# One maximum over two PSUM banks, batchwise reciprocals and a regrouped weight ring in an attention plus two-network kernel

## Chip, core and metric

One core of one Trainium2 chip. The metric is the device time of one execution in microseconds; lower is better. All stage times below come from one profiled execution of the kernel before.

## The reference

A causal attention with a decay bias (4 batches, 8 heads, 576 tokens, 64 elements a head) feeds a first feed-forward network, and that a second (512 to 2,048 to 512 elements, 2,304 tokens), all in float32:

```python
scores = scale * np.matmul(q, k.transpose(0, 1, 3, 2))
cum = np.cumsum(np.maximum(s, 0.0), axis=-1)
bias = -(cum[:, :, :, None] - cum[:, :, None, :])
scores = np.where(causal, -1000000000.0, scores + np.minimum(bias, 0.0))
attn = np.exp(scores - np.max(scores, axis=-1, keepdims=True))
attn = attn / (np.sum(attn, axis=-1, keepdims=True) + 1e-09)
x = np.matmul(attn, v)          # then (2304, 512)
h = x @ w_in;  x = (h * np.cos(h)) @ w_out
h = x @ w2_in; out = (np.maximum(h, 0.0) + np.log1p(np.exp(-np.abs(h)))) @ w2_out
```

## The kernel before

**Order.** A planner written in the kernel (class `Planner`) decides the order of everything. Each operation is an `Op` with a due value `vt`, the engines it can run on, and the tiles it reads and writes; `plan` walks through modelled time and gives each free engine the ready operation with the smallest `vt`, corrected on TensorE by what it thinks a weight load costs (`LDW`, `FX`, `then`). The due values are offsets in the table `TUNE`. Where the model sees TensorE idle, it puts in warm-up matmuls on constants: `warm` (line 415, "fillers") until the first product with v, `warmer` (line 423, tile `still`) later. All transfers are issued by SyncE (SP), one queue, in the planned order, through `dma` at line 312, and every real matmul through `mms` at line 358, so operations are told apart here by tiles and shapes.

**Attention.** `emit_attention` is called for each of the 32 heads. Every head needs its row maxima first, so each causal block is scored twice. In the first pass six matmuls (`MT`, four groups in four PSUM banks) score the five query blocks; the fifth block's 576 keys do not fit one bank of 512 columns and stand as 320 and 256 in two banks. VectorE takes one masked maximum of each piece (line 592, columns of `mx`), and line 598 combines the two of the fifth block into `mrr`. A transpose on TensorE (T, 128 columns), ScalarE (line 615) and GpSimd (line 617) turn the maxima into rows that the second pass subtracts. That pass (`STL`) scores keys by queries in four groups, two matmuls of each width (448; 128 and 320; 448; 192 and 64); ScalarE takes the exponential (line 657), GpSimd zeroes the diagonal halves (line 663), and TensorE multiplies with v, which carries a column of ones: "bank<-gs", fp32, 65 stationary columns, two passes for each of six widths. The rest is fp32r, which a row of the trace also calls f32: every value is split into a high and a low part, and three products replace one. Five of the eight PSUM banks rotate among maxima, transposes and scores (`rot`), three hold the products with v.

**Sums.** The numerator and the sum of each head go to DRAM (`adram<-gs`). After every fourth head the sums come back (`rd<-adram`), are inverted (lines 692, 693) and stored (`rdram<-rd`). `normal` then loads numerators (`uu<-adram`) and broadcast reciprocals (`wo<-rdram`), multiplies them (line 737), stores them (`xnorm<-uu`) for later use, and `emit_x` forms seven sums of blocks and their parts.

**Networks.** Each network is a two-level Strassen scheme with seven products (`PROD`, P1, P5, P6, P2, P3, P7, P4). A unit, "quad", is 42 matmuls of 384 columns with one pair of weight blocks; its weights lie in one of two ring slots (`ring`), loaded by two DMAs `rg<-wd`, a half j = 0 or 1 of 1,792 columns each, and every product needs both. The weights were converted earlier (lines 483, 485, 504, `emit_win`) and stored to `wd` in pieces of 448 KB. The products with w_out (`emit_g2`) are 384 columns wide in the first network ("bank<-rg,wo") and 512 in the second ("bank<-wo,rg", three in a row for each output block).

## Time and profile before

| | us |
|---|---|
| median of 3 runs (lowest, highest) | 959.97 (958.52, 960.05) |
| profiled execution, its span | 958.9, 957.2 |
| TensorE, weight loads, VectorE, ScalarE busy | 946.8, 866.9, 817.2, 713.3 |
| first real matmul | 7.50 |
| first matmul of the first network | 197.52 |
| start of the unbroken run of TensorE, its end | 281.92, 953.3 |

The span is one execution from its first to its last instruction; the profiled execution's own time is 1.7 us longer. Matmuls are pipelined and their records overlap, so a group's busy time says little: distances between starts say more. An idle time stands before the instruction that follows it, with what released it. The granted clock of TensorE is 1.00 in all stages.

### The profile page before, as it was taken

Reading aid. Unit: us, or ns where it says so; the run is one execution under the profiler, and the core shown is the slowest. Engines: PE = TensorE matmul, PEld = TensorE weight load, DVE = VectorE, ACT = ScalarE, POOL = GpSimd, SP = SyncE. Lnnn points to the kernel's source line nnn. Section 1 sums busy time; section 2 is a strip of 40 time slices with the busy share of each in tenths; the row PEclk is TensorE's granted clock in tenths of the full one; section 3 lists DMA queues with packets and bytes.
Section 4 is the critical chain, followed back from the end, with each engine's and each line's share of the span. In section 5 each row is a group of like instructions: output and inputs, shape, how many; then the busy total and the mean of one; then the engine's idle time right before and its main releaser. Section 6 shows DMA issues by size and latency. Waiting matters only on the chain.

```text
span 957.2 us, 15903 instructions
## 1 busy us (share of the span) xinstructions
PE 946.8 (99%) x5162; PEld 866.9 (91%) x5162; DVE 817.2 (85%) x1930; ACT 713.3 (75%) x1502; POOL 98.0 (10%) x220
## 2 busy tenths in 40 slices
PE   8999999999999999999999999999999999999998
PEld 7778878789999999999999999989899998898996
DVE  8898898959989898898897998989977788289685
ACT  5888788768778587885885877869867786377572
POOL 6444444510000000000000000000000000000000
PEclk9999999999999999999999999999999999999999
DMA  6799988988896886789858889776464445146324
GB/s 184 216 258 268 284 261 251 281 291 315 294 323 237 314 313 252 275 300 319 309 212 284 310 290 312 249 258 213 165 228 157 154 155 176 35 167 216 133 78 131
DMA packets 80972, 226.62 MB, mean 237 GB/s; under 512 B 11390, under 2 KB 22654, under 8 KB 80890
## 3 DMA queue, kind: packets, MB, share of 16 engines
q1 hardware_dynamic: 80890, 225.62, 70.0%
q8 instruction: 40, 0.66, 0.3%
q14 instruction: 42, 0.34, 0.1%
HBM read 163.49 MB, written 53.25 MB: 226 GB/s over the span
## 4 chain that ended last, share of the span: by engine, by line
PE 93%; DVE 3%; DMA 2%; SPq 1%; issue 0%; ACT 0%; DVEq 0%; ACTq 0%
PE bank L358 92%; DMA wo<-rdram 1%; SPq L312 1%; PE bank L415 1%; DMA adram<-gs 1%; DMA ae<-rdram 0%; DVE ae L812 0%; DVE gs L592 0%; DMA gs<-s 0%; DVE rg L443 0%; DVE rg L340 0%; DVE gs L438 0%; DVE ae L333 0%; DVE gs L815 0%; DVE ae L815 0%
## 5 line engine op out<-in xcount | busy, mean ns | idle before, releaser
L358 PE MATMUL bank<-xc,rg 128*128 128x384 f32 x2016 | 387.8, 335 | 3.5 <-DMA rg<-wd 2.9
L358 PEld LDWEIGHTS bank<-xc,rg 128*128 128x128 f32 x2016 | 354.4, 188 | 14.7 <-DVE ae L812 2.9
L358 PE MATMUL bank<-rg,wo 128*128 128x384 f32 x1152 | 219.5, 335 | 0.0
L358 PE MATMUL bank<-wo,rg 128*128 128x512 f32 x864 | 214.9, 392 | 0.0
L358 PEld LDWEIGHTS bank<-rg,wo 128*128 128x128 f32 x1152 | 201.1, 188 | 1.3 <-DVE rg L340 0.7
L358 PEld LDWEIGHTS bank<-wo,rg 128*128 128x128 f32 x864 | 160.9, 188 | 26.9
L358 PE MATMUL bank<-gs 128*65 128x448 f32 (+4 forms) x384 | 114.9, 410 | 0.0
L796 DVE TENSOR_TENSOR ae<-bank,ae 128x384 f32<-128x384 f32 x144 | 78.6, 552 | 41.8 <-PE bank L358 40.1
L358 PE MATMUL bank<-rg 128*128 128x448 f32 (+14 forms) x448 | 105.5, 339 | 1.8 <-DVE rg L443 1.0
L331 ACT ACTIVATE ae<-bank 128x384 f32<-128x384 f32 (+1 forms) x136 | 67.4, 499 | 44.2 <-PE bank L358 41.8
L358 PEld LDWEIGHTS bank<-rg 128*128 128x128 f32 (+5 forms) x448 | 65.8, 177 | 25.0 <-issue 11.0
L592 DVE CUSTOM_DVE_ANT_0 gs<-bank,gs 128x320 bf16<-128x320 f32 (+2 forms) x192 | 75.1, 431 | 12.1 <-PE bank L358 10.0
L331 ACT ACTIVATE rg<-gs 128x384 fp32r<-128x384 f32 x96 | 49.4, 520 | 34.9 <-PE bank L358 34.2
L657 ACT ACTIVATE gs<-bank 128x448 f32<-128x448 f32 (+1 forms) x128 | 62.2, 498 | 14.4 <-PE bank L358 9.2
L483 ACT ACTIVATE upper<-stage 128x256 f16<-128x256 bf16 x128 | 61.2, 490 | 15.1 <-DMA stage<-w 7.9
L358 PEld LDWEIGHTS bank<-gs 128*65 128x65 f32 x384 | 60.6, 195 | 5.7 <-POOL gs L663 1.4
L340 DVE TENSOR_TENSOR rg<-gs,rg 128x384 fp32r<-128x384 f32 (+1 forms) x97 | 53.0, 552 | 9.8 <-ACT rg L331 9.7
L820 DVE SCALAR_TENSOR_TENSOR ae<-ae 128x384 f32<-128x384 f32 x96 | 52.8, 553 | 9.0 <-ACT ae L819 8.3
L819 ACT ACTIVATE ae<-ae,lnb 128x384 f32<-128x384 f32 x96 | 58.1, 611 | 1.9
L331 ACT ACTIVATE rg<-ae 128x384 fp32r<-128x384 f32 x96 | 49.6, 518 | 12.4 <-DVE ae L824 9.6
L663 POOL TENSOR_SCALAR_AFFINE_SELECT gs<-gs 128x128 f32<-128x128 f32 (+1 forms) x160 | 53.7, 358 | 42.0 <-ACT gs L657 40.3
L485 DVE SCALAR_TENSOR_TENSOR wt<-stage,upper 128x256 uint32<-128x256 uint32 x128 | 51.6, 417 | 6.9 <-ACT upper L483 6.7
(96 smaller groups left out, 1200.4 us busy)
## 6 DMA issues: line engine op xcount, KB each, us to landing
rg<-wd SPq DMA_DIRECT2D x96, 896.0 KB
stage<-w SPq DMA_DIRECT2D x128, 256.0 KB
wd<-rg SPq DMA_DIRECT2D x48, 448.0 KB
uu<-qk SPq DMA_DIRECT2D x15, 576.0 KB
uu<-xdram SPq DMA_DIRECT2D x20, 384.0 KB
wd<-xc SPq DMA_DIRECT2D x16, 448.0 KB
rg<-rg SPq DMA_DIRECT2D x20, 288.0 KB
gs<-v SPq DMA_DIRECT2D x32, 160.0 KB
```

Of the source, the lines that this page charges most:

```text
L312: (G if by == POOL else nc.sync).dma_start(o, i)
L331: opts.append((ACT, act_t(n, psum), (lambda: A.activation(o, i, AF.Copy, scale=1.0 if scale is None else scale))))
L340: return [(DVE, dve_t(n), lambda: V.tensor_tensor(o, a, hi.bitcast(F32), op=ALU.subtract))]
L358: X.matmul(o, a, b, start=st, stop=sp, skip_group_check=skip)
L483: P.op(vs_ - 1 + 0.1 * z, [(ACT, act_t(256) + 45.0, lambda up=up, head=head: A.activation(up[:, :].bitcast(F16).rearrange("p (n t) -> p n ...
L485: P.op(vs_ + 0.1 * z, [(DVE, dve_t(256), lambda up=up, mid=mid, z=z: V.scalar_tensor_tensor(cv[:, z * 256:z * 256 + 256], mid, 13, up, op0 ...
L592: P.op(tx + 1, [(DVE, dve_t(w, True) + DX, free(lambda bk=bk, off=off, w=w, mo=mo, col=col, pr=pr, jk=junk[i if x < 2 else x - 2]: V.tenso ...
L657: P.op(tx + 3, [(ACT, act_t(wt, True) + AX, lambda pt=pt, bk=bk, wt=wt: A.activation(pt[:, :wt], bank[bk][:, :wt], AF.Exp))], r=[(("bank", ...
L663: P.op(tx + 4 + i, [(POOL, 160.0 + 0.8 * dw, lambda z=pt[:, off:off + dw], dw=dw: G.affine_select(out=z, in_=z, pattern=[[1, dw]], compare ...
L796: P.op(t - 80, [(DVE, dve_t(NQ, True), lambda o=o, e=et[x]: V.tensor_tensor(e, o, e, op=ALU.add))], r=done + [(ek[x], (Q, "s"))], w=[(ek[x ...
L819: P.op(te + 400, [(ACT, act_t(NQ) + 93, lambda a0=a0, a1=a1: A.activation(a1, a0, AF.Ln, bias=lnb[:, 0:1]))], r=[(k0, (tg, "e")), ("ln", 0 ...
L820: P.op(te + 700, [(DVE, dve_t(NQ), lambda a0=a0: V.scalar_tensor_tensor(a0, a0, 2.0, a0, op0=ALU.subtract, op1=ALU.mult, reverse0=True))], ...
```

## The change

- **Planner.** All numbers of `TUNE` are new. A load of v counts `LDW` = 110 ns instead of 54, `FX` is 2.5 instead of 30, and one SP transfer that depends on another becomes ready 1,000 ns later (`dd`).
- **Maxima.** PSUM is one tile of 4,096 columns. The two pieces of the fifth block stand in adjacent banks (`rot` picks the pair), and one operation of 576 columns takes their maximum. All maxima are written into `mrr` directly; `mx` and line 598 are gone.
- **Scores.** `STL` becomes 192 and 256; 320 and 64; 448; 320. The first key block is split 256 and 320 rather than 128 and 448. The first two groups are double-buffered, and the two diagonals of one group are selected in one operation on GpSimd (four a head instead of five).
- **Sums.** They are inverted once for eight heads in the first three batches; in the last batch still for four, the second time with a due value later by `late`.
- **Ring.** `wd` is laid out in two groups (`PART`): 2,048 columns for P1, P5, P6, P2 and 1,536 for P3, P7, P4. Each store to `wd` becomes two. A product waits for its own group alone.
- **Second network.** Inner blocks of w_out issue nine matmuls in one operation (three blocks of three).
- **Start.** The mask is prepared earlier on GpSimd, and two due values (`tz`, `x2nd`) move the first subtractions.

The diff, cut:

```diff
+PART = (2048, 1536)
+POS = (1, 3, 4, 2, 5, 6, 0)
...
-LDW = 107.0
+LDW = 110.0
...
-                        then = 54.0 if len(fast) > (f.load < 100.0) else LDW
+                        then = 30.0 if len(fast) > (f.load < 100.0) else LDW
...
-                    s.ready = max(s.ready, o.end + min(self.hop(e, x[0]) for x in s.opts))
+                    s.ready = max(s.ready, o.end + min(self.hop(e, x[0]) for x in s.opts) + (TUNE["dd"] if e == SP and s.opts[0][0] == SP else 0.0))
...
-AX, DX, FX = 50.0, 12.0, 30.0
+AX, DX, FX = 50.0, 12.0, 2.5
...
-    bank = [pp.tile([128, 512], F32, name=f"bank{i}", tag=f"bank{i}") for i in range(8)]
+    psum = pp.tile([128, 4096], F32, name="bank", tag="bank")
+    bank = [psum[:, i * 512:i * 512 + 512] for i in range(8)]
...
-            loads += [54.0, 0.0] if n < 0 else [max(27.0, st.shape[-1] * LDW / 128)]
+            loads += [LDW, 0.0] if n < 0 else [max(27.0, st.shape[-1] * LDW / 128)]
...
-            dma(t + 4 + z, wdram[which][i, :, j * HALF + z * 896:j * HALF + z * 896 + 896], x.bitcast(F32), r=[(("sh", h, z), tag)], w=[(("wd", which, i, j, z), 0)], by=SP)
+            for g, (a, b) in enumerate(((384, 896), (0, 384))):
+                o = g * PART[0] + (2 * j + z) * (b - a)
+                dma(t + 4 + z + 0.1 * g, wdram[which][i, :, o:o + b - a], x[:, a:b].bitcast(F32), r=[(("sh", h, z), tag)], w=[(("wd", which, i, j, z, g), 0)], by=SP)
...
-    MT = [[(4, 0, 320, 4, 0), (1, 0, 192, 1, 320)], [(3, 0, 448, 3, 0), (0, 0, 64, 0, 448)], [(2, 0, 320, 2, 0)], [(4, 320, 256, 9, 0)]]
-    STL = [[(0, 128, 0, 448)], [(0, 0, 0, 128), (2, 256, 128, 320)], [(1, 128, 0, 448)], [(3, 384, 0, 192), (4, 512, 192, 64)]]
+    MT = [[(1, 0, 192, 0), (4, 0, 320, 192)], [(4, 320, 256, 0), (0, 0, 64, 256)], [(3, 0, 448, 0)], [(2, 0, 320, 0)]]
+    STL = [[(3, 384, 0, 192), (0, 0, 192, 256)], [(0, 256, 0, 320), (4, 512, 320, 64)], [(1, 128, 0, 448)], [(2, 256, 0, 320)]]
+    AVL = [[(0, 0, 128), (3, 384, S)], [(0, 128, S), (4, 512, S)], [(1, 128, S)], [(2, 256, S)]]
...
-                    op0=ALU.add, op1=ALU.max, accum_out=m[0:pr, col:col + 1])))],
-                    r=[(("bank", bk), (bt, len(lst) - 1)), ("mask", 0)], w=[(("mx", sl, col), tg)])
-        t = at(st["max"] + 0.5)
-        mk = ("xl", 1, u % 3)
-        P.op(t, [(DVE, 115.0, lambda: V.tensor_tensor(mrr[:, 96:101], m[:, 0:5], m[:, 5:10], op=ALU.max))],
...
+                    out=jk[0:pr, :w], in0=psum[0:pr, 512 * bk + off:512 * bk + off + w], in1=mask[0:pr, mo:mo + w], scale=1.0, scalar=BIG,
+                    op0=ALU.add, op1=ALU.max, accum_out=mrr[0:pr, 96 + qi:97 + qi])))],
+                    r=[(("bank", bk), (bt, len(lst) - 1)), ("mask", 0)] + ([(("bank", rot[u, "m", 1]), ((tg, "m", 1), 1))] if qi == 4 else []), w=[(mk, tg)])
...
-        if u % 4 != 3:
+        nh = 4 if b == NB - 1 else 8
+        if u % nh != nh - 1:
             return
-        tn = at(st["norm"])
+        tn = at(st["norm"]) + (TUNE["late"] if b == NB - 1 else 0.0)
...
-        for j in range(2):
-            dma(tq - QUAD + 100 + j, ring[r].bitcast(F32)[:, j * HALF:j * HALF + HALF], wdram[which][i, :, j * HALF:j * HALF + HALF],
-                r=[(("wd", which, i, j, z), 0) for z in range(2)], w=[(("ring", r, j), Q)] + first(("ring", r, j)))
+        for g in range(2):
+            gs_ = slice(g * PART[0], g * PART[0] + PART[g])
+            dma(tq - QUAD + 100 + g * TUNE["rg"], ring[r].bitcast(F32)[:, gs_], wdram[which][i, :, gs_],
+                r=[(("wd", which, i, j, z, g), 0) for j in range(2) for z in range(2)], w=[(("ring", r, g), Q)] + first(("ring", r, g)))
...
-                P.op(tq + (y + j / 2) * h, mms(ml), r=[(("ring", r, j), Q)] + [(("xc", xi, j, t), xtag) for t in range(2)] + old, w=[(("bank", b), (Q, nm, j))])
+                P.op(tq + (y + j / 2) * h, mms(ml), r=[(("ring", r, POS[wi] < 3), Q)] + [(("xc", xi, j, t), xtag) for t in range(2)] + old, w=[(("bank", b), (Q, nm, j))])
...
+        if which and f0 < f < f1 - 1:
+            ml = [(bank[yset[m]], (hi, lo)[xt][:, m * 128:m * 128 + 128], wo[:, f, wt_], False, False, False, DM) for m in range(3) for wt_, xt in ((0, 0), (1, 0), (0, 1))]
```


**TensorE, one head in the steady part of the attention.** Names: `gs` with 65 rows of output is the product with v (its outputs' width stands behind the x), `rg` with 128 rows are maxima and scores, 32x128 is T. Before:

```order
L358 MATMUL bank_68<-rg 128x128
L358 MATMUL bank_68<-rg 128x320
L358 MATMUL bank_66<-rg 32x128
L358 MATMUL bank_68<-rg 128x320
L358 MATMUL bank_69<-rg 128x320
L358 MATMUL bank_69<-rg 128x192
L358 MATMUL bank_65<-rg 128x448 x2
L358 MATMUL bank_66<-rg 128x448
L358 MATMUL bank_66<-rg 128x64
L358 MATMUL bank_70<-gs 65x192
L358 MATMUL bank_70<-gs 65x64
L358 MATMUL bank_67<-rg 128x192 x2
```

A head of the steady part on the same engine after the change:

```order
L361 MATMUL bank<-gs 65x192
L361 MATMUL bank<-gs 65x128
L361 MATMUL bank<-rg 128x320
L361 MATMUL bank<-rg 128x256
L361 MATMUL bank<-rg 128x192
L361 MATMUL bank<-rg 128x256 x2
L361 MATMUL bank<-gs 65x448
L361 MATMUL bank<-rg 128x320 x2
L361 MATMUL bank<-gs 65x64
L361 MATMUL bank<-gs 65x448
L361 MATMUL bank<-rg 32x128
```

The two score matmuls of 128 columns (the second of the pair is the first row) are gone, 32x128 aside; the 64-column product with v stands ahead of a 448-column one rather than of a maximum, and the pairs beside the products are 256 or 320 wide.

**SP, at the end of the attention.** `adram<-gs` stores a head, `rd<-adram` reads the sums of the last four heads, `uu` and `wo` load numerators and reciprocals, `rg<-wd` fills the ring, `xnorm<-uu` stores products of VectorE. Before:

```order
L312 DMA adram<-gs 65x576 x2
L312 DMA rg<-wd_78 128x1792
L312 DMA xnorm<-uu 128x768
L312 DMA rd<-adram 128x1x18
L312 DMA uu<-adram 64x768 x2
L312 DMA wo<-rdram 64x768
L312 DMA uu<-adram 64x768 x2
L312 DMA wo<-rdram 64x768 x2
L312 DMA rg<-wd_78 128x1792
L312 DMA rdram<-rd 4x32x18
L312 DMA xnorm<-uu 128x768
L312 DMA rg<-wd_78 128x1792
```

The same queue at the same place after the change:

```order
L315 DMA adram<-gs 65x576 x2
L315 DMA rdram<-rd 4x32x18
L315 DMA rg<-wd_71 128x1536
L315 DMA uu<-adram 64x768 x2
L315 DMA wo<-rdram 64x768 x2
L315 DMA uu<-adram 64x768 x2
L315 DMA wo<-rdram 64x768 x2
L315 DMA uu<-adram 64x768 x2
L315 DMA rg<-wd_71 128x2048
L315 DMA rd<-adram 128x1x18
L315 DMA xnorm<-uu 128x768 x2
L315 DMA wo<-rdram 64x768 x2
L315 DMA rg<-wd_71 128x1536
```

The read `rd<-adram` stood two transfers behind the last heads' stores and ahead of seven loads and both ring loads; now it stands behind ten loads and the ring's first group, and the ring's second group behind it, two stores and two loads.

## Rows read from the trace of the kernel before

**Rows 1.** The page's first part: busy us (share) xinstructions by engine

```profile
PE 946.8 (99%) x5162; PEld 866.9 (91%) x5162; DVE 817.2 (85%) x1930; ACT 713.3 (75%) x1502; POOL 98.0 (10%) x220
```

**Rows 2.** By stage: window, us, busy us (instructions) of each engine, PEclk, DMA, GB/s

```profile
26.00:160.00 134.00, 133.81 (x753) 106.91 (x752) 119.49 (x410) 109.10 (x221) 62.93 (x144) 1.00 0.89 258
...
197.50:282.00 84.50, 80.99 (x458) 77.96 (x456) 71.21 (x150) 63.95 (x140) 0.00 (x0) 1.00 0.88 301
282.00:953.30 671.30, 671.30 (x3582) 634.24 (x3582) 571.58 (x1207) 495.38 (x1052) 0.00 (x0) 1.00 0.64 224
```

**Rows 3.** TensorE in time: start us, us, engine line op, count [idle before]

```profile
58.84 0.70 PE L358 MATMUL bank<-gs 128*65 128x320 f32 x2
...
59.43 0.97 PE L358 MATMUL bank<-gs 128*65 128x448 f32 x2
...
197.52 2.67 PE L358 MATMUL bank<-xc,rg 128*128 128x384 f32 x14
...
279.98 1.72 PE L358 MATMUL bank<-xc,rg 128*128 128x384 f32 x9
...
704.41 0.86 PE L358 MATMUL bank<-wo,rg 128*128 128x512 f32 x3
705.11 3.13 PE L358 MATMUL bank<-xc,rg 128*128 128x384 f32 x17
...
943.64 9.68 PE L358 MATMUL bank<-wo,rg 128*128 128x512 f32 x42
```

**Rows 4.** Weight loads (PEld) in order of time, two places of the attention

```profile
93.42 0.41 PEld L358 LDWEIGHTS bank<-rg 128*128 128x128 f32 x3 [0.27 <-issue]
...
90.41 0.31 PEld L358 LDWEIGHTS bank<-gs 128*65 128x65 f32 x2
```

**Rows 5.** TensorE in order of time, the kernel's first microseconds

```profile
7.50 1.07 PE L358 MATMUL bank<-rg 66*128 66x320 f32 x6 [1.00 <-DVE rg L443]
8.41 2.14 PE L415 MATMUL bank<-gs 128*128 128x256 bf16 x18
```

**Rows 6.** Groups by line and shape: xcount | busy us, mean ns | idle

```profile
L358 PE MATMUL bank<-xc,rg 128*128 128x384 f32 x2016 | 387.8, 335 | 3.5 <-DMA rg<-wd 2.9 <-DVE ae L333 0.3 <-DVE ae L815 0.2
...
L592 DVE CUSTOM_DVE_ANT_0 gs<-bank,gs 128x320 bf16<-128x320 f32 x64 | 31.2, 488 | 7.3 <-PE bank L358 6.3
...
L592 DVE CUSTOM_DVE_ANT_0 gs<-bank,gs 128x448 bf16<-128x448 f32 x32 | 19.9, 620 | 0.8 <-issue 0.7
...
L415 PE MATMUL bank<-gs 128*128 128x256 bf16 x114 | 16.1, 291 | 1.2 <-DVE gs L371 1.2
...
L598 DVE TENSOR_TENSOR rg<-mx 128x5 fp32r<-128x5 f32 x32 | 6.1, 191 | 0.5
```

**Rows 7.** All engines in order of time, the longest stop of the passage

```profile
214.60 0.96 DVE L737 TENSOR_TENSOR uu<-uu,wo 128x768 f32<-128x768 f32 x1 [2.54 <-DMA wo<-rdram]
...
216.76 2.91 PE L358 MATMUL bank<-xc,rg 128*128 128x384 f32 x12 [2.73 <-DMA rg<-wd]
```

**Rows 8.** The chain of waits that ended last: start us, us, what

```profile
198.31 5.26 DMA adram<-gs
...
281.92 671.41 PE bank L358 x3582
```

**Rows 9.** Waits: engine, line, releaser: us in total, times, longest

```profile
PEld bank L358 <- DVE mx L592: 5.2, 19, 0.6
...
PEld bank L358 <- DVE rg L598: 2.5, 7, 0.6
```

**Rows 10.** SyncE's queue of DMA issues in order of time, at the passage

```profile
199.19 0.58 SPq L312 DMA_DIRECT2D xnorm<-uu  x1
203.63 0.58 SPq L312 DMA_DIRECT2D rd<-adram  x1
...
208.68 0.53 SPq L312 DMA_DIRECT2D rg<-wd  x1
...
210.64 1.25 SPq L312 DMA_DIRECT2D rg<-wd  x1
```

147 lines of the change are left out of this document (82 added, 65 removed).

## The prediction

> **What bounds the kernel now.** I read the busy shares first: TensorE is busy 99% of the span, the next engine 85% [rows 1]. A busy TensorE is not one at its peak, so I then read the busy time by stage [rows 2]: TensorE fills 671.30 of 671.30 us between 282.0 and 953.3, and 80.99 of 84.50 us in the passage from the attention to the first feed-forward network. What the attention loses is hidden in overlapping records, so I took it apart by the distance between starts.
>
> The distances are these. Nine 384-column matmuls: (1.72 - 0.335) / 8 = 0.1735 us each; forty-two of 512 columns: (9.68 - 0.39) / 41 = 0.2266 each [rows 3] (0.335 is the length of one [rows 6]; 0.39 that with 128 columns more). The difference over 128 columns is 0.415 ns a column, and what is left of each matmul, 0.1735 - 384 x 0.000415, is 0.014. A stationary operand of 128 columns needs its own time: three loads of 0.19 us in 0.41 us stand (0.41 - 0.19) / 2 = 0.11 apart [rows 4]. A matmul whose stream is shorter than that waits for the next load. In the attention's fp32 product with v, 2 x 320 columns and one matmul of 128 take 59.43 - 58.84 = 0.59 us [rows 3]; less 0.067 that is 0.82 ns a column and pass.
>
> The first real matmul starts at 7.50 [rows 5], the feed-forward part at 197.52 [rows 3], so the attention has 190.0 us. A head streams 4,928 columns in 19 matmuls (2.3 us) and 3,200 columns of fp32 (2.6 to 2.7 us): about 161 us for 32 heads. Exposed loads, from the counts in the code: 111 matmuls of 128 columns at about 0.03 (3.5 us), 101 of 64 columns at 0.04 (4.1), 96 of 192 at 0.015 (1.5), 64 fp32 passes of 64 columns at 0.054 (3.5): 12.5. The fillers after 7.50 are 80 of the 114, at (2.14 - 0.29) / 17 = 0.109 us [rows 5, 6]: 8.7. The rest, 190.0 - 161.3 - 12.5 - 8.7, is about 7.5 us of waits. In the passage some 450 matmuls x 0.1735 = 78.1 of 84.4 us: 6.3 of waits, the largest 2.73 us before 216.76 [rows 7]. From 281.92 to 953.3 there are 2,718 x 0.1735 + 864 x 0.2266 = 667.4 of 671.4 [rows 8]: 4.0 over. The tail is 3.9.
>
> **The change, part by part.** The sums are made against the profiled execution, 958.9 us with its span of 957.2 and 1.7 outside; the median of the three runs, 959.97, is 1.1 above it, and the forecast stands between the two levels.
>
> *Score groups without a 128-column pair.* 64 score matmuls of 128 columns (two a head in the code) become 256 wide, whose stream (0.12) covers the next load; the other half of that block goes from 448 to 320, still above 0.11. Each 128 exposed 0.11 - 0.067 = 0.042, some less by their follower: 64 x 0.042 = 2.7 at most, 1.8 at 0.028. I take **-2.2**.
>
> *What follows the 64-column fp32 passes.* In the new order 27 of 32 are followed by another fp32 pass with 65 stationary columns, in place of an fp32r matmul with 128. If such loads were as slow as the wide ones (0.31 - 0.195 = 0.115 apart [rows 4]) nothing would be gained; if they hid wholly, 27 x 0.054 = 1.5. The nearest row says little is gained, but its two loads belong to one operand and may be held by something else, so I take the middle, **-0.9** (0 to -1.5).
>
> The Trainium skill, "TensorE: Matmul & The Clock Gate", section "LDWEIGHTS (loading the stationary operand)", has the load's time go with its columns at 1.2 a nanosecond, which is 107 ns for 128 (the row's 0.11 agrees) and an estimated 54 ns for 65. By the rule this term would be its full 1.5 and the forecast 0.6 us lower; the row's 0.115 for 65 columns speaks against it.
>
> *Maxima.* Per head VectorE loses one of six reductions and the combining step. By the 448 and the 320 wide a column costs (0.620 - 0.488) / 128 = 1.03 ns; so the 320 and the 256 wide cost 0.488 + 0.422 = 0.910, and one of 576 would cost 0.620 + 0.132 = 0.752 [rows 6]. Crossing from one bank to the next is in no row; between nothing and one more start of 0.910 - 0.752 = 0.158 (what two operations cost over one). So 0.158 + 0.191 = 0.35 a head, 11 us over the attention; at worst 0.19. VectorE fills 119.49 of 134.00 us [rows 2] and is not the bound; the gain is only where TensorE waits for it: its loads stood 5.2 us for maxima and 2.5 for the combining step [rows 9], part of which other matmuls cover. Against it: the 576-wide reduction needs two banks at once and both are held until it ends, so two of five rotating banks wait for VectorE. With the first two score groups double-buffered and one selection less on GpSimd, I take a third of the 7.5 us of waits: **-2.3**, range -4 (half) to +0.5 (the bank pair costs what the shorter work gives).
>
> *Start.* The first maxima now stand behind two subtractions on VectorE, the mask is prepared earlier, and the fillers go from 114 to 110 in the program, 34 of them again ahead of the first real matmul. What they cover is the chain from s through VectorE to the first scores, which stays: **0**, +-1.5.
>
> *Sums and queue at the passage.* Before, SP's queue stops at 199.19 until 203.63, when the reciprocal's read may go: it waits for the last head's store, 5.26 us on the chain [rows 8, 10]. Behind it stand seven loads for the normalisation, and behind those the ring's halves, issued at 208.68 and 210.64 [rows 10]; TensorE stands till 216.76 for one [rows 7], and VectorE's product waits 2.54 for the broadcast [rows 7]. Now the read goes behind ten of these loads and the ring's first group, at least ten issues of 0.6 us [rows 10] later than the store, so it no longer blocks. But the second group of the third pair stands behind that read, two stores that wait for VectorE's products, and two more loads. That group is wanted only from the fifth of a quad's seven products on, 24 matmuls or 4.2 us after its first. In the order 30 more warm-up matmuls than before stand in this stage: where they stand, TensorE was expected to be idle, and each costs at least 192 x 0.415 = 0.08: 2.4 us that stay. With 2 of small waits, 4.4 in place of 6.3: **-2** (range -4, when all go but the warm-ups; +2, when the blocked queue's 2.7 comes back at the later group and the rest stays).
>
> *Second network.* Products with w_out go in nine rather than three in a row. A three stood 705.11 - 704.41 = 0.70 for 3 x 0.2266 = 0.68: 0.02 a run [rows 3]; 46 runs less: **-0.9** (0 to -1). Nothing in this stage waits, so splitting the stores and halves there into 58 more DMAs costs nothing as long as the ring's loads land a quad ahead (SP is rarely late after 282, and TensorE never stood for it); if a group landed late it would be some 2.7 us each, as at 216.76. The batchwise inversion of the first three batches only removes small operations under TensorE's work. The tail is the same: **0**.
>
> Sum: -2.2 - 0.9 - 2.3 - 2.0 - 0.9 = -8.3, so 950.6 on the profiled level and 951.7 on the median's; I take 951.5.
>
> **The rivals.** *Waits only move.* Every wait in attention and passage is replaced by a like one (the pair of banks held, the second group late): only TensorE's own arithmetic is left, -2.2 - 0.9 - 0.9 = -4.0, 955 to 956. For it: VectorE at 89% and ScalarE at 81% of the attention [rows 2] leave little slack, and a shorter pace of TensorE tightens both. Against: the waits named by maxima are on work that goes away.
>
> *All waits go*: -4 in each of the two places, under 948. It needs the passage free of more than the warm-ups; the later second group speaks against it.
>
> *Nothing to measure*: the two-bank reduction costs as much as two, the bank pair stalls TensorE once in several heads (0.1 us a head is 3.2 us), and that eats the arithmetic: 958 to 962.
>
> *Slower.* One mechanism: second ring groups late in the passage. SP issues the third pair's second group behind two stores, and these behind products whose broadcasts have to land first; before, such a product waited 2.5 us [rows 7]. If the third and the fourth pair each wait the 2.7 us [rows 7] for it twice, that is +10.8, against -2.7 for the stall that goes and -6.3 for the other terms: some 962. It decides as soon as the passage has over 8 us more waits than before. Against it: the group is wanted 4.2 us after the quad begins.
>
> **How the numbers follow.** Forecast, 948 to 955: 0.52. All waits go: 0.12. Waits only move: 0.16. Nothing to measure: 0.11. Slower: 0.09. About 0.2%, 1.9 us, is what a measurement of this kernel can tell from no change, so faster is 0.52 + 0.12 + 0.16 = 0.80, same 0.11, slower 0.09. The range runs from 945.5 (the sum with the better bounds of waits, -13 or so, cut where 0.03 is left) to 959.0, which takes in the moved waits and some of no change.
>
> **What would show it.** In the changed kernel: no 128-column score matmuls, the distance between the attention's first matmul and the first of 384 columns at about 184.5 us instead of 190.0; the maximum's 576-wide row near 0.75 us (0.9 would take away half of VectorE's gain); no stop of SP between 199 and 204; the passage (first 384-column matmul to the start of the long unbroken run) with about 4 us of idle TensorE and warm-ups; the long run shorter by under 1 us. Wrong would be: TensorE's loads waiting for the wide reduction more than the 7.7 us of before; a wait for the ring of over 2 us in the third or fourth pair; fillers at the start reaching past 24 us, which would mean that VectorE's reordered start costs more than I allow.

## The result and the profile after

The changed kernel took 969.13 us (median of four runs, 967.85 to 971.28) against 959.89 of the kernel before on the same chip: a ratio of 1.0102, 95% interval 1.008 to 1.0124. It is 9.2 us slower where 8.5 less was forecast. The profiled execution took 968.4 us, 9.5 more than that of before.

The page's first part, and then the windows by stage (columns as in [rows 2]; the windows are shifted by what each stage starts later):

```profile
PE 950.6 (98%) x5186; PEld 867.4 (90%) x5186; DVE 818.0 (85%) x1825; ACT 710.4 (73%) x1502; POOL 100.2 (10%) x189
```

```profile
26.00:160.00 134.00, 132.16 (x746) 104.29 (x745) 115.83 (x325) 106.83 (x216) 67.02 (x121) 1.00 0.89 252
200.50:284.00 83.50, 81.99 (x481) 80.04 (x480) 72.43 (x151) 63.49 (x139) 0.00 (x0) 1.00 0.91 311
284.00:956.00 672.00, 667.30 (x3554) 628.30 (x3554) 571.75 (x1208) 494.34 (x1056) 0.00 (x0) 1.00 0.67 223
```

VectorE has 105 fewer instructions, and in the attention 115.83 busy us instead of 119.49: its work did get shorter. But TensorE, which filled the long last stage to the last hundredth [rows 2], is now idle for 4.7 of its 672 us, and for 1.6 us more in the attention.

Busy time hides part of such losses, so I took TensorE's course apart with the prediction's own distances: for each kernel they are summed over its matmuls in their real order, and what a matmul starts later than that sum is time lost (the time of fillers and warm-ups is counted as lost too). The sum itself fell from 918.4 to 915.0 us. By stage the losses are, in us:

| stage | before | after | difference |
|---|---|---|---|
| to the second real matmul | 7.58 | 8.21 | +0.6 |
| next 8 us of its own work (to 28 us) | 10.01 | 11.74 | +1.7 |
| next 12 us (28 to 43) | 0.61 | 3.10 | +2.5 |
| rest of the attention | 5.59 | 7.19 | +1.6 |
| passage, to the 450th feed-forward matmul | 6.43 | 5.33 | -1.1 |
| first network from there | 0.33 | 6.17 | +5.8 |
| border and second network | 3.97 | 5.78 | +1.8 |

The losses add up to +13.0, with -3.4 of work +9.6, which is the difference of the two profiles. Three places carry it: the start (+4.8), the rest of the attention (+1.6, where the maxima are), the first network and what follows it (+7.6). Each loss, here and below, comes from one profiled execution. The kernels below that keep the order of the changed kernel in the networks lost between 5.4 and 9.4 us in the first one, so differences of 2 us there say little.

**The start.** VectorE, GpSimd and then TensorE after the change (start us, us, engine, line, operation):

```profile
10.63 1.59 DVE L588 TENSOR_TENSOR rg<-uu,rg 64x576 fp32r<-64x576 f32 x1
12.25 0.75 DVE L590 SCALAR_TENSOR_TENSOR rg<-uu,rg 64x576 fp32r<-64x576 f32 x1
13.04 0.36 DVE L610 CUSTOM_DVE_ANT_0 gs<-bank,gs 128x192 bf16<-128x192 f32 x1
13.54 0.76 DVE L610 CUSTOM_DVE_ANT_0 gs<-bank,gs 128x576 bf16<-128x576 f32 x1
```

```profile
9.95 1.66 POOL L394 TENSOR_SCALAR_AFFINE_SELECT xc<-cst 32x1152 fp32r<-32x1152 f32 x1
```

```profile
14.46 0.71 PE L361 MATMUL bank<-rg 66*128 66x192 f32 x4 [1.75 <-DVE rg L610]
```

The two subtractions stand ahead of the first maxima, so TensorE stands 1.75 us for the maxima. The first subtraction takes 1.59 us, where the same operation takes 0.75 in f2_maxfirst, further down. It runs beside a fill on GpSimd (a select that fills a tile from constants, the middle line), and that is about 0.84 us of the stop. The windows behind that stop show more than the stop (columns as in [rows 2], the granted clock is the third figure from the right):

```profile
14.00:16.00 2.00, 1.54 (x8) 1.15 (x8) 1.93 (x9) 0.00 (x0) 0.00 (x0) 0.72 0.56 162
16.00:18.00 2.00, 2.00 (x12) 1.37 (x12) 0.49 (x2) 0.78 (x2) 0.00 (x0) 0.50 0.04 8
18.00:20.00 2.00, 2.00 (x18) 1.76 (x17) 1.90 (x7) 0.30 (x1) 0.00 (x0) 0.93 0.12 12
```

The granted clock falls to 0.50, the lower of its two levels, and 12 matmuls fill the 2 us in which 20 stand at full clock (f1_fill below). Before the change the clock was 1.00 there.

**28 to 43 us.** VectorE, GpSimd and TensorE:

```profile
26.94 2.31 DVE L588 TENSOR_TENSOR rg<-uu,rg 64x1152 fp32r<-64x1152 f32 x1
30.87 2.29 DVE L590 SCALAR_TENSOR_TENSOR rg<-uu,rg 64x1152 fp32r<-64x1152 f32 x1
```

```profile
26.89 1.15 POOL L405 TENSOR_SCALAR_AFFINE_SELECT rg<-cst 32x1152 fp32r<-32x1152 f32 x1
30.80 1.15 POOL L394 TENSOR_SCALAR_AFFINE_SELECT rg<-cst 32x1152 fp32r<-32x1152 f32 x1
```

```profile
34.01 0.77 PE L361 MATMUL bank<-xc 66*128 66x320 f32 x4 [0.94 <-DVE rg L610]
```

Each subtraction of the second pair starts within 0.1 us of a fill on GpSimd and takes 2.3 us. The same form takes 1.35 us where no such fill runs, as both did in the kernel before. The 576-wide maximum is queued behind the second of them.

**The maxima.** The groups of VectorE and GpSimd, and TensorE's waits for maxima (us in total, times, longest), which answer to [rows 6] and [rows 9]:

```profile
L610 DVE CUSTOM_DVE_ANT_0 gs<-bank,gs 128x576 bf16<-128x576 f32 x32 | 24.2, 756 | 4.1 <-PE bank L361 1.2 <-ACT gs L647 1.0 <-ACT gs L673 0.2
```

```profile
PEld bank L361 <- DVE rg L610: 12.6, 37, 1.1
PE bank L361 <- DVE rg L610: 3.1, 3, 1.7
```

The operation over two banks takes 0.756 us, where 0.752 was worked out; crossing the banks costs nothing. Yet the loads wait 12.6 us for maxima, not 5.2 + 2.5. Most of that, 11.1 us, lies between 43 and 197 us, where the waits of before for maxima and combining step come to 6.6.

**The first network.** SyncE's queue, ScalarE, VectorE and TensorE at the largest stop:

```profile
352.04 2.73 SPq L315 DMA_DIRECT2D stage<-w  x3
356.67 0.33 SPq L315 DMA_DIRECT2D rg<-wd  x1
357.09 4.63 SPq L315 DMA_DIRECT2D wd<-rg  x4
362.04 0.32 SPq L315 DMA_DIRECT2D rg<-wd  x1
362.46 4.14 SPq L315 DMA_DIRECT2D stage<-w  x3
368.28 0.33 SPq L315 DMA_DIRECT2D rg<-wd  x1
```

```profile
371.06 0.49 ACT L483 ACTIVATE upper<-stage 128x256 f16<-128x256 bf16 x1 [3.84 <-DMA stage<-w]
```

```profile
371.58 0.43 DVE L485 SCALAR_TENSOR_TENSOR wt<-stage,upper 128x256 uint32<-128x256 uint32 x1 [2.74 <-ACT upper L483]
371.93 0.55 DVE L817 TENSOR_TENSOR ae<-bank,ae 128x384 f32<-128x384 f32 x1
```

```profile
373.80 3.39 PE L361 MATMUL bank<-xc,rg 128*128 128x384 f32 x18 [1.39 <-DVE ae L817]
```

Read it backwards. TensorE waits 1.39 us for VectorE to add up a bank (L817). VectorE stood 2.74 us behind a conversion of weights (L485), which waited for ScalarE, which stood 3.84 us for a staged weight (`stage<-w`); that load was issued behind ring groups (`rg<-wd`) and stores (`wd<-rg`). The weights are those of a later part, here w_out of the first network itself (from 390 us on they are the second network's): weights staged ahead hold up the engines that empty the banks of the products now running. ScalarE's waits for staged weights between 282 and 600 us, before and after:

```profile
ACT upper L483 <- DMA stage<-w: 4.4, 6, 1.2
```

```profile
ACT upper L483 <- DMA stage<-w: 20.0, 15, 3.8
```

The loads do not land more slowly than before (median between 4 and 5 us from issue in both), but they are issued late. Of the 74 loads of staged weights in that stretch 23 went out more than 1 us after their buffer was free, 118 us late together; before, 15 of 73 with 47 us. In the queue 11 of the late ones, with 63 us, stood behind a group of the ring, and before none did. Behind stores stood 9 each time, with 49 us and with 33.

### The profile page after: what moved, and what is told of

It reads as the page before. It is cut to its first block, busy times and chain, and to the rows that moved or that the text cites. A ratio compares the mean times of both kernels' runs of the same rounds, so it can differ in the third digit from the quotient of the medians.

```text
span 966.7 us, 15848 instructions
## 1 busy us (share of the span) xinstructions
PE 950.6 (98%) x5186; PEld 867.4 (90%) x5186; DVE 818.0 (85%) x1825; ACT 710.4 (73%) x1502; POOL 100.2 (10%) x189
## 4 chain that ended last, share of the span: by engine, by line
PE 76%; DVE 10%; DMA 7%; ACT 4%; issue 2%; SPq 0%; POOL 0%; DVEq 0%; ACTq 0%
PE bank L361 76%; DMA stage<-w 3%; DMA wd<-rg 3%; DVE rg L343 2%; DVE xc L343 1%; DVE ae L833 1%; DVE ae L817 1%; DVE gs L836 1%; ACT rg L334 1%; ACT ae L831 1%; DVE gs L610 1%; ACT ae L832 1%; DVE ae L836 1%; DVE wt L485 1%; DMA rg<-wd 1%
## 5 line engine op out<-in xcount | busy, mean ns | idle before, releaser
L361 PE MATMUL bank<-xc,rg 128*128 128x384 f32 x2016 | 379.8, 335 | 3.8 <-DVE ae L817 1.9
L361 PEld LDWEIGHTS bank<-xc,rg 128*128 128x128 f32 x2016 | 353.3, 188 | 11.4 <-DVE ae L817 4.0
L361 PE MATMUL bank<-wo,rg 128*128 128x512 f32 x864 | 207.3, 391 | 0.0
L361 PE MATMUL bank<-rg 128*128 128x320 f32 (+13 forms) x444 | 103.1, 341 | 3.7 <-DVE rg L610 2.2
L817 DVE TENSOR_TENSOR ae<-bank,ae 128x384 f32<-128x384 f32 x144 | 79.6, 554 | 26.4 <-PE bank L361 22.9
L610 DVE CUSTOM_DVE_ANT_0 gs<-bank,gs 128x576 bf16<-128x576 f32 (+5 forms) x160 | 74.7, 488 | 16.3 <-PE bank L361 7.2
L673 ACT ACTIVATE gs<-bank 128x448 f32<-128x448 f32 (+2 forms) x128 | 60.8, 500 | 19.8 <-PE bank L361 18.9
L683 POOL TENSOR_SCALAR_AFFINE_SELECT gs<-gs 128x128 f32<-128x128 f32 (+2 forms) x128 | 57.7, 463 | 70.2 <-ACT gs L673 67.5
L343 DVE TENSOR_TENSOR rg<-gs,rg 128x384 fp32r<-128x384 f32 (+1 forms) x97 | 53.5, 555 | 11.3 <-ACT rg L334 11.0
L334 ACT ACTIVATE rg<-ae 128x384 fp32r<-128x384 f32 x96 | 49.8, 519 | 17.7 <-DVE ae L845 11.3
L485 DVE SCALAR_TENSOR_TENSOR wt<-stage,upper 128x256 uint32<-128x256 uint32 x128 | 53.3, 427 | 11.3 <-ACT upper L483 10.3
```

Source lines behind the costliest of these rows:

```text
L334: opts.append((ACT, act_t(n, psum), (lambda: A.activation(o, i, AF.Copy, scale=1.0 if scale is None else scale))))
L343: return [(DVE, dve_t(n), lambda: V.tensor_tensor(o, a, hi.bitcast(F32), op=ALU.subtract))]
L361: X.matmul(o, a, b, start=st, stop=sp, skip_group_check=skip)
L485: P.op(vs_ + 0.1 * z, [(DVE, dve_t(256), lambda up=up, mid=mid, z=z: V.scalar_tensor_tensor(cv[:, z * 256:z * 256 + 256], mid, 13, up, op0 ...
L610: P.op(at(st["max"] + MD) + 1 if qi == 4 else tx + 1, [(DVE, dve_t(wt_, True) + DX, free(lambda bk=bk, off=off, w=wt_, mo=mo, qi=qi, pr=pr ...
L673: P.op(tx + 3, [(ACT, act_t(wt, True) + AX, lambda pt=pt, bk=bk, wt=wt: A.activation(pt[:, :wt], bank[bk][:, :wt], AF.Exp))], r=[(("bank", ...
```

## Experiments: the start

A kernel planned anew after an edit gets another order everywhere. So most kernels here keep the changed kernel's own planned order and alter one thing in the finished list (`order`, line 977).

**f1_fill**: 16 more filler matmuls after the first 32.

```diff
     order = P.plan()
+    more = [order[[x for x in pe if order[x].fn is warm][0]]] * 16
+    order[at_[0]:at_[0]] = more
```

> The changed kernel in its own order, with 16 more fillers on TensorE where it stands idle for 1.75 us ahead of the first maxima's second bank pair (14.46 us); nothing else moves. Theory 'the low clock costs': the granted clock stays at 1.00 through 14 to 20 us and TensorE is 1 to 2 us earlier at 40 us; the end 967 to 968. Rival 'VectorE is what is late there': the clock stays up, TensorE does its work sooner and waits for VectorE as long as before, and nothing comes back by 40 us.

**f2_maxfirst**: the first head's two subtractions moved behind its maxima.

```diff
+    order = [o for o in order if o not in mv]
+    x = max(x for x, o in enumerate(order) if o.eng == DVE and ((("xl", 1, 0), 0) in o.writes))
+    order[x + 1:x + 1] = mv
```

> The changed kernel in its own order, with only the first head's two subtractions on VectorE moved behind that head's five maxima. Theory 'VectorE's order at the start': TensorE's stop before 14.46 shrinks from 1.75 to under 0.5 us, the clock stays at 1.00, 2 to 4.5 us come back by 40 us, and later stages stay as they are: 964.5 to 967. Rival 'the order decides but any move is given back': the gain at 40 us is gone by the end of the attention at 201 us.

Windows of f1_fill, then of f2_maxfirst:

```profile
16.00:18.00 2.00, 2.00 (x20) 1.80 (x20) 1.33 (x5) 1.08 (x2) 0.00 (x0) 1.00 0.00 0
```

```profile
16.00:18.00 2.00, 1.15 (x10) 0.86 (x8) 1.90 (x8) 0.00 (x0) 0.00 (x0) 1.00 0.34 60
```

Both keep the clock at 1.00. With fillers the loss up to 28 us is 10.76 instead of 11.74, so the low clock costs about 1 us. Three later kernels say the same without a filler: e2_netnum, j_ring and j_store have the stop of 1.75 us too (1.73 to 1.74), but not the fall behind it, and they lost 1.0 to 1.1 us less up to 28 us. Here j_ring:

```profile
16.00:18.00 2.00, 2.00 (x20) 1.78 (x20) 1.34 (x5) 1.08 (x2) 0.00 (x0) 1.00 0.04 8
```

So the length of the stop does not settle whether the clock falls: behind the same stop it fell to 0.50 in f4_onestore, g_pair, i_stage and k_stores.

With the maxima first the loss up to 28 us is 9.40, under the kernel before, and the attention ends at 197.95 instead of 200.96. The times, 968.52 and 967.46 (ratios 1.0092 and 1.0086), don't show it: the first network lost 9.4 and 8.5 in these profiles.

**i_fills** and **j_fills**: f2_maxfirst with the two fills elsewhere in GpSimd's order, ahead of its first selects (11.7 to 13.9 us) or behind two of them (21.7 to 24.1).

```diff
+    for o in [o for o in pool if ((("augk", 1), 0), "z") in o.writes or (("augq", 1, 0), 0) in o.writes]:
+        order.remove(o)
+        order.insert(order.index(after_) + 1, o)
+        after_ = o
```

> f2_maxfirst (first head's subtractions behind the first maxima) with two GpSimd fills of 1.15 us each (32 partitions, lines 394 and 405, for the second pair's buffers) moved ahead of GpSimd's first selects, into its idle time at 12 to 19 us. Theory (the second pair's subtractions take 2.30 us and not 1.35 because these fills run beside them): both subtractions take 1.35, TensorE's loss between 28 and 40 us falls from 3.1 to 1.2 or less, attention ends 1.5 to 2 us earlier than in f2_maxfirst (197.9), time 965 to 966. Rival (VectorE's order alone makes that loss): the subtractions get shorter, the loss stays over 2.5.

> f2_maxfirst with the two GpSimd fills behind GpSimd's first two selects, so at about 21.6 to 24 us, where VectorE runs maxima and not subtractions (i_fills put them at 11.7 to 13.9, beside the first head's subtraction, which took 1.66 us instead of 0.75, and TensorE's clock fell). If the overlap with fills is what lengthens subtractions: all of them 1.35 and 0.75, the start's gain of f2_maxfirst (2.4 us to 28 us) and that of i_fills at 28 to 40 us (1.1 us) both stand, attention ends at 196 to 197, time 965 to 967 (the first network's loss varies by some 3 us). If each gain is handed on to the next wait, attention ends at 198 as in f2_maxfirst.

i_fills, VectorE and GpSimd, and the window with the fall:

```profile
12.87 1.66 DVE L588 TENSOR_TENSOR rg<-uu,rg 64x576 fp32r<-64x576 f32 x1
```

```profile
12.77 1.15 POOL L394 TENSOR_SCALAR_AFFINE_SELECT rg<-cst 32x1152 fp32r<-32x1152 f32 x1
```

```profile
20.00:24.00 4.00, 4.00 (x24) 3.25 (x22) 2.82 (x3) 1.89 (x6) 3.86 (x5) 0.59 0.32 91
```

The second pair's subtractions take 1.35 us in both kernels and the loss from 28 to 43 us falls from 3.1 to 2.0: the overlap is shown, and the delay went where the fill went. In i_fills the first head's subtraction takes 1.66 instead of 0.75 us, TensorE's stop grows from 0.85 to 1.75 us, and the clock falls to 0.59. In j_fills all subtractions are short and the clock stays, but GpSimd's selects come later and TensorE waits for one:

```profile
25.99 1.02 PE L361 MATMUL bank<-gs 128*65 128x448 f32 x2 [1.10 <-POOL gs L683]
```

Attention ended at 200.0 and 199.4, not 196 to 197; the times were 967.37 and 967.97. The start's losses are real, but they don't add up: what one order takes off VectorE's chain, the next wait in line gives back in part. VectorE has little room there (busy 18.8 of the 20 us from 8 to 28 in f2_maxfirst).

**g_both** and **h_unsplit** also moved the second pair's second subtraction behind its maximum, in the orders of g_pair and e1_halves. In the finished list it then stands behind the load of the third pair's queries and keys, so VectorE waited 4.6 and 4.8 us for that load and worked on the wrong pair's values. They took 979.71 and 966.86 us and say nothing on that move.

> As g_pair, and the first head's two VectorE subtractions stand behind the first maxima and the second pair's second subtraction behind its one-operation maximum. If the start and the ring are two separate losses, both go: TensorE's loss up to 40 us falls by some 3 to 5 us and the first network's by 3 to 8, together 958 to 961, about the kernel before. If the start's gain is only handed to a later wait, the time is that of g_pair within 1 us.

> The kernel with ring and stores unsplit (as e1_halves, planned anew) and the same moves of the three subtractions. e1_halves took 964.4. If the start's loss is real in this order too, 960 to 961; if later waits take it up, 964. No version with these parts is expected under 957, since the changed kernel's own work is only 3.4 us shorter than that of the kernel before.

**e3_maxfirst** asks for f2's order in the planner (the subtractions read the maxima's tag, `tz` 900) and plans anew.

> Puts VectorE's two subtractions of the first head behind the first head's maxima again, as before the change; nothing else. In the changed kernel TensorE stands 1.75 us at 14.46 for the first maximum, its granted clock falls to 0.50 between 16 and 18 us, and by 40 us it is 4.6 us later than before. Theory 'VectorE's order at the start': the 1.75 us and the low clock go and 3 to 4.6 us come back, 964.5 to 966. Rival 'the start is late for another reason' (the two-bank maximum, the key chain behind 25 us): under 1.5 us come back.

It took 971.21 us. The start up to 43 us lost 11.3 instead of 14.8, the rest of the attention 12.2 instead of 7.2: the new plan gave more back than the start gained.

## Experiments: the maxima

**f3_twoop** splits the 576-wide maximum in place into 320, 256 and the combining step; **e4_twoop** plans the same anew.

```diff
+        for y, (a, w) in enumerate(((0, 320), (320, 256))):
+            V.tensor_tensor_reduce(out=jk[0:pr, :w], in0=psum[0:pr, 512 * bk + off + a:512 * bk + off + a + w], in1=mask[0:pr, mo + a:mo + a + w], scale=1.0, scalar=BIG,
+                                   op0=ALU.add, op1=ALU.max, accum_out=mxp[0:pr, y:y + 1])
+        V.tensor_tensor(acc, mxp[0:pr, 0:1], mxp[0:pr, 1:2], op=ALU.max)
```

> The changed kernel in its own order, with the 576-wide maximum split in place into 320, 256 and a small combining operation (0.485 + 0.42 + about 0.15 us for 0.756). It prices the one operation alone. If VectorE's length is what TensorE waits for, 32 x 0.3 = 10 us more work on VectorE cost 3 to 8 us in the attention, 972 to 977; if the waits are set by order and by banks that are held, under 1.5 us.

> Undoes the one operation over two banks alone: the fifth block has two maxima of 320 and 256 columns and one small combining operation again, in the same two adjacent banks. Theory 'the pair of banks held by one long operation': TensorE's waits for maxima (12.6 us of its weight loads' idle time against 7.7 before) fall to 8 or less and 2 to 4 us come back, 965 to 967. Rival 'shorter work on VectorE is what it is, and the waits come from the order': VectorE has 11 us more to do and the time stays or rises by up to 3 us, 969 to 972.

f3_twoop took 974.9 us (ratio 1.0176). Its attention lost 30.1 us from the first matmul on, against 22.0 of the changed kernel. Its waits for maxima (L307 are the pieces of the split one):

```profile
PEld bank L367 <- DVE rg L616: 20.3, 35, 1.5
PE bank L367 <- DVE rg L616: 6.8, 18, 1.0
PEld bank L367 <- DVE mx L307: 3.8, 14, 0.8
PE bank L367 <- DVE mx L307: 1.8, 2, 1.4
```

The split adds 0.35 us a head, 11 us in all, by the prediction's rows. Measured it is 0.40, or 13 us: pieces of 0.488 and 0.424 and a combining step of 0.167 for one of 0.756, and each reduction has a short read of 0.08 behind it, which the prediction did not count. Of this 8.1 arrived at the end of the attention. So in this order TensorE waits for VectorE, and most of what one operation saves over three arrives. e4_twoop lost 22.0 as well in the attention (971.64 us in all; 2.2 more in the passage and 2.7 more in the first network): a plan made for two operations hides them. The gain is there only against an order that was made for the shorter work.

## Experiments: the first network

**e1_halves** undoes both splits (stores of 896 columns, ring by halves), planned anew. **k_stores** undoes the ring's groups alone. **e2_netnum** keeps both splits and gives the staging its due numbers of before.

```diff
-            for g, (a, b) in enumerate(((384, 896), (0, 384))):
...
+            dma(t + 4 + z, wdram[which][i, :, j * HALF + z * 896:j * HALF + z * 896 + 896], x.bitcast(F32), r=[(("sh", h, z), tag)], w=[(("wd", which, i, j, z), 0)], by=SP)
...
-            dma(tq - QUAD + 100 + g * TUNE["rg"], ring[r].bitcast(F32)[:, gs_], wdram[which][i, :, gs_],
+            dma(tq - QUAD + 100 + j, ring[r].bitcast(F32)[:, j * HALF:j * HALF + HALF], wdram[which][i, :, j * HALF:j * HALF + HALF],
```

```diff
-            backlog=2151.19, hz=611921.0, xs=2844.35, xm=0.387013, xn=0.116304, xa=1968.85, xb=5717.21, hold=298.794, lead=5569.67,
+            backlog=1774.68, hz=493273.0, xs=2089.92, xm=0.337949, xn=0.169259, xa=2216.83, xb=3252.51, hold=187.083, lead=4071.79,
```

(`li`, `lo` and `ul` likewise.)

> Undoes the ring alone: the weights' stores are 896 columns wide in one piece again and the ring is loaded in two halves that every product needs; all numbers of the plan stay. In the changed kernel the first network (282 to 620 us) loses about 8 us more than before, with ScalarE waiting 20 us for staged weights. Theory 'small transfers': the twice as many and narrower stores keep the queue and the transfer engines longer, so staged weights land late; then this kernel gets back 6 to 8 us, near 962, and ScalarE's wait for staged weights falls to about 5 us. Theory 'due numbers': the conversions were planned closer to their use and the layout is innocent; then the time stays within 2 us of 969 and the waits for staged weights stay at 15 us or more.

> Gives the network part the due numbers of the kernel before (due times of the weight conversions, of the loads and stores around the networks, backlog and hold) and leaves all structure of the change. Theory 'due numbers': the 8 us that the first network lost come back, 961 to 963. Theory 'small transfers': they stay, 967 to 970, with ScalarE's wait for staged weights still over 15 us.

> The ring loaded by halves again, as in e1_halves, but each store of a staged half still in two parts (512 and 384 columns), as in the changed kernel; planned anew, as e1_halves is. e1_halves took 964.4 and lost 2 us between TensorE's 450th and last matmul of the first network, the changed kernel 6 and the other kernels with both splits 5 to 11. If the ring's groups make that loss: loss 1 to 3.5, time 963 to 966. If the doubled stores make it: loss 6 or more, time 968 to 972. In between, both carry part of it.

They took 964.35, 969.17 and 967.19 us (ratios 1.0041, 1.0094 and 1.0089; the interval of k_stores is 1.0058 to 1.012). The first network lost 1.99, 8.81 and 1.53: the staging's due numbers are not the cause. ScalarE's waits in e1_halves, then k_stores:

```profile
ACT upper L483 <- DMA stage<-w: 6.6, 4, 3.6
```

```profile
ACT upper L483 <- DMA stage<-w: 7.5, 6, 2.5
```

So the first network's loss goes with the ring's groups. All kernels with halves show it: before 0.33, e1_halves 1.99, k_stores 1.53, h_unsplit 2.49, i_best 1.26, with at most one stage load late behind a half of the ring. The fifteen with groups lost 5.4 to 21.2.

The time gains less by the halves than the first network does, because the newly planned kernels with halves lose more behind it: some 6.6 to 8.4 us at the border and in the second network, where the changed kernel lost 5.8 and the kernel before 4.0. In e1_halves TensorE waits there for a half (waits between 590 and 640 us):

```profile
PEld bank L361 <- DMA rg<-wd: 2.1, 1, 2.1
```

Both networks together come to some 8 to 10 us in these kernels, 12.0 in the changed one and 4.3 before. By the times, both splits undone are worth some 0.6% (the interval of e1_halves, 1.0025 to 1.0057, lies below that of the changed kernel). The groups alone undone are not told from it: the interval of k_stores overlaps. So the traces point at the groups and the times also at the doubled stores: k_stores is 2.8 us over e1_halves by medians, but not in the profiled runs (965.86 and 966.62). What each split costs stays open.

How the groups do it was tried in SyncE's queue, the order of the compute engines unchanged. **f4_onestore** writes one store at the first one's place and lets the ring's loads gather:

```diff
-                (G if by == POOL else nc.sync).dma_start(o, i)
+            elif alt:
+                nc.sync.dma_start(*alt)
```

> The changed kernel in its own order, with each pair of stores of converted weights made one store of 896 columns (as before the change), while the ring's two groups are gathered from it in rows of 512 and 384 columns instead of 2,048 and 1,536. Theory 'the doubled stores': SyncE's time for these stores between 282 and 590 us falls from 37.5 to about 14 us, ScalarE's wait for staged weights from 20 to under 8 us, 4 to 7 us come back: 962 to 965. Rival 'narrow pieces on either side' or 'the second group's place': ScalarE's wait stays over 12 us and under 2 us come back.

970.36 us, loss 11.4. SyncE spent 13.6 instead of 37.5 us on issuing stores, and 19.6 instead of 12.8 on the ring's loads. It didn't help: it isn't the issuing time of the stores alone.

**g_pair** puts the first group's load next to the second's:

```diff
+            order.pop(x)
+            order.insert(lim - 1, a)
```

> The changed kernel in its own order on every compute engine; only SyncE's queue differs: the first group of each weight-ring half is loaded directly ahead of its second group, so that the two stand as a pair and the queue stops once per half for TensorE and not twice with stage loads between. Queue theory: the late stage loads of the first network go, ScalarE's waits for staged weights fall from 20 us to under 8, TensorE's loss between its 450th and its last matmul of the first network falls from 6 to 11 us to 3 or less, and the time is 962 to 964. Rival (the loss there comes from the conversions' and casts' places on ScalarE and VectorE): waits for staged weights stay at 16 to 22 us and the time stays at 968 to 970.

975.63 us. The waits for staged weights stayed (20.1 us in the same window), and TensorE waited for the ring in the passage:

```profile
PEld bank L361 <- DMA rg<-wd: 3.3, 1, 3.3
```

The pair stands where the later group stood, so the first group came late; the passage lost 11.3 us instead of 5.3.

**i_stage** puts each load of a staged weight directly behind the conversion that frees its buffer:

```diff
+        y = max([order.index(d) for d in o.deps] + [-1]) + 1
+        if y < x:
+            order.insert(y, order.pop(x))
```

> The changed kernel in its own order on the four compute engines; in SyncE's queue alone, the loads of staged weights from the passage to the end of the first network stand directly behind the conversion that frees their buffer, that is by 1 to 12 places ahead of ring-group loads and stores that wait for TensorE, ScalarE and VectorE. In the changed kernel 23 such loads left over 1 us after their buffer was free, together 118 us. Queue theory (late stage loads are what the first network loses): these lates fall to under 50 us, ScalarE's waits for staged weights from 20 us to under 8, TensorE's loss in the first network from 6 to 2 or less, time 963 to 965. Rival (ring groups that arrive late in their turn, since they are now behind the stage loads): waits for staged weights fall, but TensorE waits for ring groups instead, and the time stays within 967 to 972.

This decided the question, against my theory. The loads were issued about 0.2 us after their buffer was free on average, one of 23 late ones was left, and ScalarE's waits for them fell from 20.0 to 11.5 us. Yet the first network lost 12.5 us (time 975.13). VectorE and ScalarE now waited for the stores (after the change 2.8 and 2.3 us):

```profile
DVE rg L343 <- DMA wd<-rg: 12.0, 7, 3.7
ACT rg L334 <- DMA wd<-rg: 5.9, 5, 2.3
```

**j_ring** and **j_store** give the ring's loads or the stores to GpSimd's queue:

```diff
-            (G if by == POOL else nc.sync).dma_start(o, i)
+            (via or nc.sync).dma_start(o, i)
```

> The changed kernel with every instruction in its own order; the loads of the ring's groups are issued from GpSimd's queue and not from SyncE's, so that a group that waits for TensorE holds no staged-weight load or store behind it. Theory (SyncE issues in order, and what waits holds all that stands behind it; i_stage put the stage loads first and the stores came late instead): late stage loads fall from 23 to about the 9 held by stores, without more late stores; ScalarE's waits for staged weights from 20 to 8 to 12 us, the first network's loss from 6 to 1 to 3 us, time 963 to 966. Rival (the split transfers themselves, twice as many and smaller, are slower, or GpSimd issues slower than SyncE): the loss stays at 6 to 12 and the time at 968 to 975.

> As j_ring, but the stores of the staged halves go to GpSimd's queue, and the ring's loads stay in SyncE's. By the same theory the 9 late stage loads behind stores go and the 11 behind ring groups stay: ScalarE's waits for staged weights 10 to 15 us, first network's loss 2 to 5, time 965 to 967. If stores are late because GpSimd issues slowly, VectorE and ScalarE wait more than the 5 us of the changed kernel for stores, and the time is over 969.

977.2 and 982.5 us, losses of 8.3 and 21.2; j_ring also lost 12.0 us in the passage, where the changed kernel lost 5.3. In j_ring nearly every late stage load stood behind a store (13 of 16, with 84 us); in j_store behind a ring group (16 of 17, with 87): whichever kind stays holds them. In j_store the stores themselves came late (VectorE waited 16.0 us for them). A second issuing engine didn't help. The Trainium skill, "DMA: Bandwidth & Descriptors", section "Issuing engines are not separate DMA queues", says that such transfers share the same DMA engines and that only issuing time is saved; these runs agree that a second issuer brings nothing, and none shows the sharing itself.

What is shown: with the ring in groups, loads of staged weights stand behind them in the queue, and the engines that empty TensorE's banks wait for those loads; when one kind of transfer was moved out of the way, another came late. It isn't the place of one kind alone, the issuing time of the stores, the due numbers or the shared queue alone. That the circle of transfers and engines has less slack with groups is my reading of this and not shown by itself. What stays open is whether the groups do it through SyncE's order or through the order that the planner then gives ScalarE and VectorE; a kernel with groups and the compute order of the halves was not tried.

**i_best** joins what helped: e1_halves with f2's and i_fills' moves.

> Ring and stores unsplit (the plan of e1_halves, 964.4), the first head's subtractions behind the first maxima and the two fills early, all other orders as in e1_halves. If start, second pair and first network are three separate losses: 964.4 less 2.5 less 1.9, that is 959.5 to 961, level with the kernel before. If a gain of the attention is handed to a later wait: 962 to 964.

963.37 us (ratio 1.0047, interval 1.0028 to 1.0067), 1.0 under e1_halves where 3.5 to 5 were expected if the losses were separate. The first network lost 1.26, but its fills stand beside the first head's subtraction as in i_fills, and the stop there is 1.76 us (16.73 to 18.49); the clock stays at 1.00 behind it, unlike in i_fills. No kernel here beats the kernel before.

## Why the prediction was wrong

- **Start: 0, +-1.5; measured +4.8.** The step says that the fillers cover a chain "which stays". It doesn't stay: two subtractions moved into it, and TensorE stood 1.75 us. What the step had no term for is the fill beside the first of them (0.84 us), the clock behind that stop (about 1 us) and the second pair, where subtractions and fills meet (+2.5). Its own sign of being wrong came true: the fillers reach to 29.2 us, where 24 was the limit.
- **Maxima: -2.3, worst +0.5; measured +1.6 (the rest of the attention).** The price of the operation was right (0.756 for 0.752). The failing step is to take a third of the waits off because VectorE's work gets shorter. The waits depend on the order; TensorE's loads waited 12.6 us, more than the 7.7 that the prediction named as its own refutation. f3_twoop shows that the saved work counts in that order, e4_twoop that another order hides the longer work. The attention as a whole did not get shorter: its last products ended about 3 us later, and the first 384-column matmul came 189.7 us after the first real one, where 184.5 was to show the gain.
- **Second network, "nothing in this stage waits, so splitting ... costs nothing": measured +5.8 and +1.8.** This step failed most. It looked at whether the ring's groups land in time, and they do: TensorE waits for none in the passage or the first network. But the staging of later weights, of both networks, shares SyncE's queue with them, and TensorE waits for the engines that do it. The step's premise that SyncE is rarely late there did not hold for these loads: even before, 15 went out over 1 us late. TensorE did not wait for them then (0.33 us lost), and that was taken for room. How the groups take it away is open, as said. The 46 runs saved were to bring 0.9 us: what stands between the runs of w_out products beyond their distances fell from 0.84 to 0.32 us, so about 0.5.
- **Scores and followers: -3.1; the summed distances fell by 3.4.** These are the prediction's own distances over the real order, so they confirm the counts and not the price of each. One price can be read: after the change a matmul behind a 64-column fp32 pass starts 0.104 to 0.113 us after it in all 27 places, though its stream needs only about 0.05. So the followers' -0.9 was about nothing, as the nearest row had said; with 0.11 there the sums fall by 3.0. The Trainium skill's rule on weight loads ("TensorE: Matmul & The Clock Gate", "LDWEIGHTS (loading the stationary operand)") would have made one term 0.6 larger. The trace does not agree for these fp32 operands: the rule's estimate is 54 ns where the 0.104 to 0.113 us stand, and the loads of 65 columns last 0.196 us on average, those of 128 last 0.188 to 0.191.
- **Passage: -2; measured -1.1.** The reciprocal's read no longer holds SyncE's queue from 199 to 204 us (it stops from 199.3 to 202.0 for the last head's store), and the warm-ups stay, as said. The slower rival's mechanism, second groups late in the passage, didn't occur after the change; g_pair is what it looks like.
- **The rivals.** "Waits only move" came nearest in kind, but it kept the arithmetic as a floor under the gain. "Slower" gave 962 for another reason. None let new waits appear in the first network, so 969 lay outside all of them.

## What to carry over

A stage in which TensorE waits for nothing has shown that its order fits, and not that it has slack: before splitting transfers there, count what else shares their queue, how late it already is and who waits for it, and give the split a price of a few late loads. When an operation gets shorter under a planned order, price its gain by what the new order makes TensorE wait for, not by the waits of the old one. At a start, look for what a moved operation runs beside, and allow for the clock falling behind an added stop, which it did in some kernels and not in others.

## What the hardware showed

- A VectorE subtraction of two SBUF operands takes 2.30 us instead of 1.35, or 1.66 instead of 0.75, when a GpSimd select that fills a tile from constants (1.15 us) runs beside it, so nearly the whole fill is added. Beside a memset the longer one still took 1.35 us (j_fills, at 24.34). When the subtraction starts first the other engine pays: in f2_maxfirst two selects at 18.98 took 2.61 us together. A maximum that reads PSUM isn't slowed: in i_fills one of 320 columns beside such a fill took 0.49 us, as elsewhere [rows 6]. The Trainium skill, "SBUF — State Buffer", section "Terms", says that the two engines share a port pair that one of them holds for a whole instruction while the other is blocked; the subtractions and the selects agree, those beside a memset show no such block.
- After a stop of 1.75 us at 12.7 to 14.5 us the granted clock was 0.72, 0.50 and 0.93 in the next three windows of 2 us, and 0.59 at 20 to 24 in i_fills after another of 1.75; after the 0.85 us of f2_maxfirst it stayed at 1.00. After stops of 1.73 to 1.76 us it stayed at 1.00 in e2_netnum, j_ring, j_store and i_best, so the stop alone does not decide it; what else does is open.
- One reduction across two PSUM banks costs as much as its columns say: 0.756 us for 576, with 0.488 for 320 and 0.620 for 448 in one bank [rows 6].
- A weight load of 65 fp32 columns holds up the next matmul as one of 128 columns does: 0.104 to 0.113 us apart, 27 times of 27.
